# A gated layer in blocks of 1024 rows, with the seven-product form for the down product too

## The chip, the cores and the metric

One core of a Trainium2 chip runs the kernel. The metric is the device time in microseconds (us). Before the change it is 1163.14 us, the median of three runs (1162.55 to 1168.49). The engines are TensorE (PE in the profile; PEld is its weight load), VectorE (DVE), ScalarE (ACT), GpSimd (POOL) and SyncE (SP), whose queue issues nearly all DMA transfers.

## What is computed

Two layers, each an FNet mixing (a real part of a two-dimensional DFT by matrices) and a gated unit. S is 2048, D is 640, F is 1728.

```python
def _A_ref(x, dft_seq_re, dft_seq_im, dft_hid_re, dft_hid_im):
    a = jnp.einsum("bsd,ed->bse", x, dft_hid_re)
    b = jnp.einsum("bsd,ed->bse", x, dft_hid_im)
    return jnp.einsum("ts,bse->bte", dft_seq_re, a) - jnp.einsum("ts,bse->bte", dft_seq_im, b)

def _B_ref(x, w_gate, w_up, w_down):
    g = jnp.einsum("bsd,df->bsf", x, w_gate)
    u = jnp.einsum("bsd,df->bsf", x, w_up)
    return jnp.einsum("bsf,fd->bsd", _sigmoid(g) * u, w_down)

x = A_x
x = x + _A_ref(_layernorm(x), ...)
x = x + _B_ref(_layernorm(x), B_w_gate, B_w_up, B_w_down)
x = x + _A_ref(_layernorm(x), ...)
x = x + _B_ref(_layernorm(x), B_w_gate, B_w_up, B_w_down)
```

## The kernel before

**Numbers.** Every fp32 operand is split into two fp16 parts, HI and LO, and a product takes three matmuls (HI by HI, HI by LO, LO by HI: `PASSES`). The split is one ScalarE instruction (HI) and one VectorE instruction (LO).

**Mixing.** `sequence` and `hidden` use the symmetries of the DFT matrices ("folds" of the rows and columns, `fold_...`), so that mixing is short. That the matrices have these symmetries is tested while the kernel runs: `load_rows`, `load_cols` fetch pieces of the matrix into one of two rooms, `test_rows` and `test_cols` (VectorE, lines 1299, 1300, 1302 and 1316 on) subtract, and `square_rest` (ScalarE, line 1277) sums the squares. At the end a flag is set, and if it is bad, a second general program runs. `test_w` also checks the range of the weights.

**Gated unit.** The 2048 rows are taken in four blocks of 512 (`SB`). The first block in each layer is plain: `gate_up(b, j)` computes a tile of 128 columns of gate and up, 30 matmuls of 512 columns (line 1051), for each of 13 tiles j and a tail of 64 + 64 columns. The other three blocks use a form of Strassen and Winograd: halves of 256 rows and the two sets gate and up give a 2 by 2 product, computed in seven products instead of eight. `seven(b, j)` runs it for two tiles j and j + 1 side by side, each part for the one and then for the other (54 matmuls of 256 columns a tile, in `products`, line 1097; the tail is line 1180). The sums of weights (`make_sums`, GpSimd, lines 998 to 1001) are made once and kept in DRAM; the sums of rows are made by `pair_combine` on VectorE. Three of the products share one PSUM chain: `snap` (ScalarE, line 1101) copies the running sum out between them, before the next one adds to the same bank. VectorE adds the sums (1133, 1134), ScalarE takes the sigmoid (1143), VectorE multiplies (1153, 1155), and ScalarE and VectorE split the result (1164, 1165).

**Down.** `down` computes 128 rows by 640 columns, in two halves of 320, over all of F: 82 matmuls of 320 columns (line 1244) for 128 rows. VectorE adds the result to the rows (line 1259), and in the second layer they are stored.

**Memory and order.** Everything lies in one SBUF tensor `big`, in units of 128 columns. Some tiles have fixed places; the rest come from `Slots`, which picks, among a few free places, the one that was freed longest ago. A step is a group of matmuls; every other piece of work is put at a step by hand (`at(u, f, ...)`), and each engine executes its own list in that order, waiting only for what it needs. The opening has an order of its own (`OPENING`).

Of the kernel before, what the change touches and what calls it, by code (L numbers as in the profile page):

```python
# [16 lines left out]
P = 128  # L17
S = 2048
# [29 lines left out]
WMAX = 16.0  # L48
# [12 lines left out]
UNITS = 388  # L61
# [5 lines left out]
XTU = NT * 2  # L67
WDU = (NF + 1) * 5
FIX = XU + 2 * XTU + WDU


class Slots:

    LOOK = {4: 2, 5: 6}

    def __init__(self, big):
        self.big = big
        self.live = {}  # L80
        self.freed = {}
        self.clock = 0
        self.close = False

    def take(self, n, high):
        taken = sorted(self.live.values())
        if self.close:

            ends = [FIX] + [d for _, d in taken]
            free = [(a, b) for a, b in zip(ends, [c for c, _ in taken] + [UNITS]) if a + n <= b]  # L90
            assert free, f"no room for {n}: {taken}"
            if high:
                a = [a for a in range(UNITS - n, FIX - 1, -n) if all(a + n <= c or d <= a for c, d in taken)][:high]
                if a:
                    return self.new(min(a, key=lambda a: max(self.freed.get(u, 0) for u in range(a, a + n))), n)
                a = max(b for _, b in free) - n
            else:
                a = min((a for f in free for a in {f[0], f[1] - n}),
                        key=lambda a: (max(self.freed.get(u, 0) for u in range(a, a + n)), a))
            return self.new(a, n)  # L100
        found = []
        for i in range(UNITS):
            a = UNITS - (i + 1) * n if high else FIX + i * n
            if a < FIX or a + n > UNITS:
                break
            if all(a + n <= c or d <= a for c, d in taken):
                found.append(a)
                if len(found) == self.LOOK.get(n, 3):
                    break
        if not found:  # L110
            found = [a for a in range(FIX, UNITS - n + 1) if all(a + n <= c or d <= a for c, d in taken)][:1]
        assert found, f"no room for {n}: {taken}"
        age = lambda a: max(self.freed.get(u, 0) for u in range(a, a + n))
        return self.new(min(found, key=age), n)

    def new(self, a, n):
        s = Slot(self.big[:, a * UNIT : (a + n) * UNIT], (a, a + n))
        self.live[id(s)] = s.span
        return s

    def give(self, s):
        self.clock += 1
        del self.live[id(s)]
        for u in range(*s.span):
            self.freed[u] = self.clock


class Slot:
# [9 lines left out]
PASSES = ((HI, (HI, LO)), (LO, (HI,)))  # L138

# [27 lines left out]
    wshi 0 0, evhi 1 1 1, wld 4 0, ev 1 1 2, ev 1 1 1, wshi 0 1, hid 0 1, hid 1 0, evhi 1 1 0, wslo 0 1, ev 1 1 0,  # L167
    difhi 1, hid 2 1, dif 1, hid 2 0, sum 0, add 0, wshi 4 0, nst 0, sum 1, nst 1, hidev 1 0, hidev 2 0, npow 0,
    add 1, wld 4 1, hid 3 1, nst 2, nst 3, nscale 0, hid 1 1, nrm 0, nrm 1, nhi 0, nhi 1, hidev 3 1, nlo 0,
    hidev 1 1, nlo 1, wld 3 1, tp 0, wslo 2 1, tp 1, wslo 0 0, npow 1, tpl 0, tpl 1, nscale 1, mid, tph 1, tph 0,  # L170
    hidev 2 1, wld 3 0, wshi 3 1, nrm 2, nhi 2, wslo 2 0, nlo 2, gu 0 0, tp 2, gu 1 0, nrm 3, wslo 3 1, tpl 2,
    tph 2, midhi, middif, nhi 3, wshi 4 1, nlo 3, tp 3, wslo 4 0, tph 3, wslo 4 1, gu 2 0, tpl 3, wshi 3 0,
    wslo 3 0, gu 0 1, gu 1 1, gu 2 1"""
# [24 lines left out]
def folded(ctx, tc, pool, dram, big, acc, flag, x, ct, wh, wg, wu, wc, wd, out):  # L198
# [4 lines left out]
    half = pool.tile([P, 4], F32, name="half")  # L203
# [3 lines left out]
    small = [pool.tile([P, 2, 24], F32, name=f"small{i}") for i in range(8)]  # L207
# [7 lines left out]
    turn = [0]  # L215
    n_sum, n_max = [0], [0]

    def scratch():
        turn[0] += 1
        return small[turn[0] % len(small)]  # L220

    nc.vector.memset(half, -0.5)
# [17 lines left out]
    def start():  # L240
        nc.gpsimd.memset(dsum, 0.0)
        nc.gpsimd.memset(cmax, 0.0)

# [12 lines left out]

    steps = []
    jobs = defaultdict(list)

    def at(u, f, *a):  # L260
        jobs[max(0, int(u // 1))].append((u, f, a))
# [3 lines left out]
    def take(n, *key, high=False):  # L265
        key = key if len(key) > 1 else key[0]
        assert key not in held, key
        held[key] = slots.take(n, high)
        return held[key]

    def fixed(at, n, *key):

        assert key not in held, key
        held[key] = Slot(big[:, at * UNIT : (at + n) * UNIT], None)
        return held[key]

    def drop_fixed(*key):
        del held[key]
# [56 lines left out]
    def load_x(i, g):  # L335

        turned = g in (GB, GC)
        v = fixed(FIX - WDU + 10 * i + 5 * (g - GB), 5, "xr", i, g).f32 if turned else X[:, 4 * i + g, :]
# [23 lines left out]
    def turned_squares(i, g):  # L362
# [3 lines left out]
        drop_fixed("xr", i, g)  # L366
# [22 lines left out]
    stats = {}  # L389
# [6 lines left out]
    def rstd_power(t, n, on=nc.gpsimd):  # L396
        c = [t[:, :n, k] for k in range(24)]
        on.tensor_scalar(c[14], c[13], 1.0, EPS, op0=OP.mult, op1=OP.add)
        nc.gpsimd.tensor_tensor(c[15], c[14], half[:, :n], op=OP.pow)
# [18 lines left out]
    def norm_scale(r, n=1, on=nc.gpsimd):  # L418
        t = stats.pop((r, n))
        rstd(t, n, XS, on)  # L420

    def norm_stats_act(r):

        t, junk = stats[r], take(5, "junk").f32
# [5 lines left out]
    def norm_pair(r):  # L430
        t = stats[r, 2] = scratch()
        for q in range(2):
            stats[r + q] = t[:, q, :]

    def norm_stats_dve(r):
        t = stats[r]
        for h in range(2):
            nc.vector.bn_stats(t[:, 6 * h : 6 * h + 6], X[:, r, h * EH : (h + 1) * EH])
        nc.vector.bn_aggr(t[:, 12:14], t[:, 0:12])

    def norm_apply(r, on_act=False):
        t = stats.pop(r)

        xn = fixed(XU + XTU + 10 + 5 * r, 5, "xf", r).f32
# [1366 lines left out]
```

## Time and profile before

| | |
|---|---|
| median of the runs | 1163.14 us |
| the profiled execution, first to last instruction | 1160.1 us |
| TensorE busy | 97% |
| VectorE busy | 64% |
| ScalarE busy | 44% |
| GpSimd busy | 13% |
| DMA, mean | 187 GB/s, 216.40 MB |

The profile is of one execution. A grouped line names the line of the kernel, the engine, the operation, output and input, shapes, the count, the busy time in us, the mean of one in ns, and the idle time before it with what ended it. A row of the windows gives, for a stretch of time, the busy us and the count of PE, PEld, DVE, ACT and POOL, the granted clock (1.00 is full), the mean busy share of the DMA engines and what they moved in GB/s. Matmuls overlap, so the mean ns of one is not the time from one to the next.

### The profile page before, as it was taken

Reading aid. Unit: us, or ns where it says so; the run is one execution under the profiler, and the core shown is the slowest. Engines: PE = TensorE matmul, PEld = TensorE weight load, DVE = VectorE, ACT = ScalarE, POOL = GpSimd, SP = SyncE. Lnnn points to the kernel's source line nnn. Section 1 sums busy time; section 2 is a strip of 40 time slices with the busy share of each in tenths; the row PEclk is TensorE's granted clock in tenths of the full one; section 3 lists DMA queues with packets and bytes.
Section 4 is the critical chain, followed back from the end, with each engine's and each line's share of the span. In section 5 each row is a group of like instructions: output and inputs, shape, how many; then the busy total and the mean of one; then the engine's idle time right before and its main releaser. Section 6 shows DMA issues by size and latency. Waiting matters only on the chain.

```text
span 1160.1 us, 22627 instructions
## 1 busy us (share of the span) xinstructions
PE 1127.3 (97%) x8784; PEld 859.6 (74%) x8784; DVE 737.6 (64%) x1636; ACT 508.2 (44%) x1094; POOL 147.6 (13%) x269
## 2 busy tenths in 40 slices
PE   6699999999999999999999999999999999999997
PEld 2467446788878887888776744678887888788874
DVE  7996888768748666685428557747974557525530
ACT  6864575155515653365204312325542555225410
POOL 2312674201002010100000001000100001000000
PEclk9999999999999999999999999999999999999999
DMA  8418698959596977679203552678859682767301
GB/s 278 136 46 242 243 358 267 280 163 234 156 222 185 242 215 187 199 236 261 70 24 108 189 150 81 185 230 251 245 155 252 205 282 93 168 207 246 115 18 38
DMA packets 225621, 216.40 MB, mean 187 GB/s; under 512 B 68034, under 2 KB 181851, under 8 KB 225502
## 3 DMA queue, kind: packets, MB, share of 16 engines
q1 hardware_dynamic: 224862, 212.23, 62.3%
q0 software_dynamic: 640, 2.62, 0.6%
q8 instruction: 71, 1.16, 0.4%
q14 instruction: 48, 0.39, 0.1%
HBM read 171.03 MB, written 30.40 MB: 174 GB/s over the span
## 4 chain that ended last, share of the span: by engine, by line
PE 81%; DMA 3%; POOL 2%; DVE 1%; issue 1%; ACT 1%; SPq 0%; POOLq 0%; DVEq 0%; ACTq 0%
PE acc L1097 36%; PE acc L1244 31%; PE acc L1051 8%; PE acc L855 2%; PE acc L1180 2%; PE acc L773 1%; DMA big<-kept_w 1%; DMA big<-in_ct 1%; POOL big L999 1%; POOL big L1000 1%; DMA kept_s<-big 1%; DVE big L238 0%; POOL big L998 0%; POOL big L1001 0%; DMA big<-kept_s 0%
## 5 line engine op out<-in xcount | busy, mean ns | idle before, releaser
L1097 PE MATMUL acc<-big 128*128 128x256 f16 x4212 | 462.9, 273 | 1.4 <-DVE small L416 1.4
L1097 PEld LDWEIGHTS <-big 128*128 128x128 f16 x4212 | 411.9, 98 | 49.9 <-DMA big<-kept_w 1.7
L1244 PE MATMUL acc<-big 128*128 128x320 f16 x2624 | 357.7, 299 | 0.0
L1244 PEld LDWEIGHTS <-big 128*128 128x128 f16 x2624 | 256.8, 98 | 99.7
L1101 ACT ACTIVATE big<-acc 128x256 f32<-128x256 f32 x312 | 116.1, 381 | 200.1 <-PE acc L1097 198.5
L1051 PE MATMUL acc<-big 128*128 128x512 f16 (+1 forms) x990 | 176.5, 340 | 0.6 <-ACT big L236 0.4
L1051 PEld LDWEIGHTS <-big 128*128 128x128 f16 x990 | 96.5, 98 | 79.6 <-ACT big L236 0.8
L1277 ACT ACTIVATE big<-big 128x768 f32<-128x768 f32 (+8 forms) x104 | 79.4, 764 | 130.4 <-DVE big L1302 94.8
L1165 DVE TENSOR_TENSOR big<-big 128x512 f16<-128x512 f32 x78 | 53.8, 690 | 110.7 <-ACT big L1164 110.7
L1259 DVE SCALAR_TENSOR_TENSOR big<-acc,big 128x320 f32<-128x320 f32 x64 | 28.4, 484 | 88.3 <-PE acc L1244 88.2
L238 DVE SCALAR_TENSOR_TENSOR big<-big 128x640 f16<-128x640 f32 (+6 forms) x81 | 64.5, 834 | 2.8 <-ACT big L236 2.2
L1143 ACT ACTIVATE big<-big 128x512 f32<-128x512 f32 x78 | 47.9, 627 | 39.2 <-DVE big L1134 39.1
L1299 DVE TENSOR_TENSOR big<-big 128x256 f32<-128x256 f32 x64 | 26.6, 416 | 52.6 <-DMA big<-in_ct 51.3
L236 ACT ACTIVATE big<-big 128x640 f16<-128x640 f32 (+7 forms) x81 | 50.7, 665 | 17.0 <-DMA kept_s<-big 7.7
L1134 DVE TENSOR_TENSOR big<-big,acc 128x512 f32<-128x512 f32 x78 | 53.1, 681 | 3.2 <-PE acc L1097 3.0
L1153 DVE SCALAR_TENSOR_TENSOR big<-acc,big 128x256 f32<-128x256 f32 x78 | 32.6, 418 | 33.4 <-PE acc L1097 28.4
L1164 ACT ACTIVATE big<-big 128x512 f16<-128x512 f32 x78 | 48.8, 626 | 7.8 <-DVE big L1155 6.8
L855 PE MATMUL acc<-big 128*128 128x321 f16 (+3 forms) x324 | 49.0, 300 | 1.1 <-DVE big L238 1.1
L855 PEld LDWEIGHTS <-big 128*128 128x128 f16 (+3 forms) x324 | 28.2, 95 | 20.3 <-issue 7.7
L509 ACT ACTIVATE big<-big 128x384 f16<-128x384 f32 (+2 forms) x48 | 28.9, 647 | 31.4 <-DVE big L491 17.6
L1066 DVE SCALAR_TENSOR_TENSOR big<-acc,big 128x512 f32<-128x512 f32 x26 | 17.9, 687 | 35.0 <-PE acc L1051 28.5
L773 PE MATMUL acc<-big 128*128 128x256 f16 (+5 forms) x288 | 36.9, 288 | 2.6 <-DVE big L664 2.6
(183 smaller groups left out, 978.7 us busy)
## 6 DMA issues: line engine op xcount, KB each, us to landing
big<-kept_w SPq DMA_DIRECT2D x125, 320.0 KB
big<-kept_s SPq DMA_DIRECT2D x75, 512.0 KB
big<-in_ct SPq DMA_DIRECT2D x256, 128.0 KB
big<-kept_w SPq DMA_DIRECT2D x78, 192.0 KB
kept_w<-big SPq DMA_DIRECT2D x41, 320.0 KB
big<-in_ct SPq DMA_DIRECT2D x32, 256.0 KB
kept_s<-big SPq DMA_DIRECT2D x13, 512.0 KB
big<-in_wg SPq DMA_DIRECT2D x16, 320.0 KB
```

The costliest lines, as they stand in the source:

```text
L236: nc.scalar.activation(dh, src, AF.Copy, scale=s)
L238: nc.vector.scalar_tensor_tensor(dl, src, s, dh, op0=OP.mult, op1=OP.subtract)
L773: nc.tensor.matmul(o, xv[:, 384 * xp + c0 : 384 * xp + c0 + n], moving(r, cps[cp]), start=(i % 2 == 0 and r == 0 and xp == HI and cp == HI ...
L855: nc.tensor.matmul(ps[:m, :EC], z[:, at : at + m], w[:, 384 * wp : 384 * wp + EC], start=(d == 0 and zp == HI and wp == HI), stop=(d == ND ...
L1051: nc.tensor.matmul(ps, w[wp][:, d * P : (d + 1) * P], xt[:, xp, :], start=(d == 0 and wp == HI and xp == HI), stop=(d == ND - 1 and wp == LO))
L1097: nc.tensor.matmul(ps, wt, xt, start=start and n == 0, stop=n == len(todo) - 1, skip_group_check=not start)
L1101: nc.scalar.activation(dst, ps, AF.Copy)
L1134: nc.vector.tensor_tensor(v, v, other, op=OP.add)
L1164: nc.scalar.activation(s.parts[HI], v, AF.Copy)
L1165: nc.vector.tensor_tensor(s.parts[LO], v, s.parts[HI], op=OP.subtract)
L1244: nc.tensor.matmul(held["pd", e][0][:, :EH], held["ht", j].parts[hp][:, i * P : (i + 1) * P], held["w", 2, j].parts[wp][:, e * EH : (e + 1 ...
L1277: nc.scalar.activation(v, v, AF.Square, accum_out=new_sum()[:p])
```

## The change

1. **Blocks of 1024 rows.** There are two blocks; in the seven-product form the halves have 512 rows, so each of the seven products is a series of matmuls of 512 columns. Column tiles j = 0 to 5 of the first block are still plain (`JC`), for both halves; tiles 6 to 12 of the first block and all 13 of the second are in the form. `seven(j)` is six steps and `four(j)` a seventh, which comes in the midst of the next tile. That makes 20 tiles in the form for each layer.
2. **Three downs in the form.** In the first block of the first layer `down` stays as it was in arithmetic. In the other three, pairs of column tiles (6 pairs of F), the halves of rows and the two halves of 320 columns give a 2 by 2 product. It runs product by product: `stage(h, s, i)` is product s of 7 for 128 rows, 18 matmuls of 320 columns; the rest of F (tile 12 and the tail) adds 5 for each 128 rows by 320 columns. The sums of the down weights are made on GpSimd (`make_forms`), split, and kept in DRAM in the first layer; the sums of activations are made by VectorE (`sums_of`) and GpSimd (`third_sum`), and each product's factor is split (`split_form`).
3. **Row pairs.** `pair_combine` of the second block is on GpSimd. Transposed rows have one buffer (`XW`), not two.
4. **Places.** No tile but the rows has a fixed place; every `take` gets the next number of a table, `PLACES`.
5. **Order.** Steps carry a duration, and other work is put at a time (`when(t, f, ...)`) on the sum of these durations.
6. **Tests.** Three rooms in place of two, loaded two turns ahead and not one; a row of a piece has 256 columns, not 128. The range of most weights is tested where they are first loaded, in the first layer, and the upper bound is 4, not 16.

The diff, cut to its core:

```diff
-WMAX = 16.0
+WMAX = 4.0
+JC = 6
+PLACES = """
+311 389 198 205 250 365 289 115 268 85 207 357 321 147 295 91 341 180 106 362 217 97 225 220 352 336 101 255
...
+    def take(self, n):
+        a = self.places.pop(0)
...
-    def part_one(b, j):
-        chain, kc = bank()
-        other, ko = bank()
-        chain = chain[:, :256]
...
+    def seven(j):
+        def one():
+            held["chain", j] = bank()
+            products(held["chain", j][0], j, [("G0", "x00")], start=True)
+        def one_post():
+            snap(take(4, "y", 0, j).f32, held["chain", j][0])
+        def five():
+            held["other", j] = bank()
+            products(held["other", j][0], j, [("S1", "T1")], start=True)
+        def five_post():
+            take(8, "hw", j)
+            snap(hw(1), held["other", j][0])
+        def two():
+            held["first", j] = bank()
+            products(held["first", j][0], j, [("G1", "x01"), ("GM", "x0M")], start=True)
+        def two_post():
+            ps, k = held.pop(("first", j))
+            nc.vector.tensor_tensor(hv(0), hv(0), ps, op=OP.add)
+            free_bank(k)
+            due(2, lambda: sigmoid(hv(0)))
+        def six():
+            products(held["chain", j][0], j, [("S2", "T2")])
...
+        return [(n * 0.2158, f, g) for n, f, g in ((6, one, one_post), (6, five, five_post), (9, two, two_post),
+                                                   (6, six, six_post), (9, three, three_post), (9, seven, seven_post))]
...
+    def make_forms(n):
+        b12, b11, b21, b22 = (held["fr", n].f32[:, k * EH : (k + 1) * EH] for k in range(4))
+        v = take(10, "ft", n).f32
+        t1, t3, t2, t4 = (v[:, k * EH : (k + 1) * EH] for k in range(4))
+        nc.gpsimd.tensor_tensor(t1, b12, b11, op=OP.subtract)
+        nc.gpsimd.tensor_tensor(t3, b22, b12, op=OP.subtract)
+        nc.gpsimd.tensor_tensor(t2, b22, t1, op=OP.subtract)
+        nc.gpsimd.tensor_tensor(t4, b21, t2, op=OP.subtract)
+        absmax(wmax[:, 2, n : n + 1], held["fr", n].f32)
...
+    TAKES = ((0, 0), (0, 1), (0, 0), (1, 0), (0, 1), (1, 0), (1, 1))
+    INTO = (("chain", 0), ("other", 0), ("other", 3), ("chain", 1), ("other", 1), ("chain", 3), ("chain", 2))
+    REST = {1: 0, 4: 1, 6: 2}
...
+    def stage(h, s, i, final):
+        into, k = INTO[s]
+        fresh = s in (0, 1, 2)
+        def mm():
+            half, second = TAKES[s]
+            if fresh:
+                held[into, "d", i] = bank()
+            ps = held[into, "d", i][0]
...
+            if s in REST:
+                rest_products(ps, REST[s] // 2, i, REST[s] % 2, False)
+        def post():
...
+            rows_add(h, k // 2, i, k % 2, ps)
+            if s in (1, 4, 6):
+                del held[into, "d", i]
+                free_bank(bk)
```

Two places show how instructions have moved. The first is ScalarE's list in the seven-product form of the first layer, beside the folds of the second quarter of rows. Before (1101 is a snap, 1164 the HI part of a result, 621 and 623 are folds, 1277 a squaring of a test, 1143 the sigmoid):

```order
L1101 ACTIVATE big<-acc_69 128x256
L1101 ACTIVATE big<-acc_65 128x256
L1164 ACTIVATE big<-big 128x512
L621 ACTIVATE big<-big,coef_89,quad_77 128x321
L623 ACTIVATE big<-big,quad_77 128x320
L1277 ACTIVATE big,dsum<-big 128x768
L1101 ACTIVATE big<-acc_67 128x256
L1101 ACTIVATE big<-acc_346 128x256
```

After, in the second block of the first layer (1112 is a snap, 1115 the sigmoid, 1415 a squaring, 240 the HI part of a form of the down weights, 624 and 626 are the folds):

```order
L1112 ACTIVATE big<-acc_65 128x512
L240 ACTIVATE big<-big 128x3x320
L1415 ACTIVATE big,dsum<-big 128x768
L1112 ACTIVATE big<-acc_69 128x512
L240 ACTIVATE big<-big 128x4x320
L1115 ACTIVATE big<-big 128x512
L1415 ACTIVATE big,dsum<-big 128x768
L1112 ACTIVATE big<-acc_69 128x512
L624 ACTIVATE big<-big,coef_86,quad_77 128x321
L626 ACTIVATE big<-big,quad_77 128x320
L1112 ACTIVATE big<-acc_66 128x512
```

Snaps have twice the columns, stand one by one, and have splits of the forms and squarings between them. The second place is VectorE's list there. Before (1133, 1134 are sums of products, 1299, 1300, 1302 a test, 1153, 1155 the products of gate and up, 1165 a LO part):

```order
L1133 TENSOR_TENSOR big<-big 128x256
L1134 TENSOR_TENSOR big<-big,acc_346 128x512
L1299 TENSOR_TENSOR big<-big 128x256
L1300 TENSOR_TENSOR big<-big 128x256
L1302 TENSOR_TENSOR big<-big 128x128 x2
L1153 SCALAR_TENSOR_TENSOR big<-acc_69,big 128x256
L1155 SCALAR_TENSOR_TENSOR big<-big 128x256
L1165 TENSOR_TENSOR big<-big 128x512
```

After (1158, 1173, 1185 are sums of products, 1188 and 1202 the products of gate and up, 1336 is a sum for the down form, 1445, 1446, 1448 a test, 667 a fold, 242 the LO part of a form):

```order
L1158 TENSOR_TENSOR big<-big,acc_65 128x512
L1188 SCALAR_TENSOR_TENSOR big<-big 128x512
L1336 TENSOR_TENSOR big<-big 128x512 x2
L1445 TENSOR_TENSOR big<-big 128x256
L1446 TENSOR_TENSOR big<-big 128x256
L1448 TENSOR_TENSOR big<-big 128x128 x2
L1202 SCALAR_TENSOR_TENSOR big<-acc_64,big 128x512
L667 TENSOR_TENSOR big<-big 128x2x321
L667 TENSOR_TENSOR big<-big 128x2x320
L242 SCALAR_TENSOR_TENSOR big<-big 128x4x320
L1173 TENSOR_TENSOR big<-big,acc_66 128x512
L1336 TENSOR_TENSOR big<-big 128x512
```

The sums for the down form and the LO parts of the forms of the weights have joined the list between the additions that free PSUM banks (1158, 1173, 1202).

1187 lines of the change are left out of this document (656 added, 531 removed), and 31 rows, old and new, of the table PLACES.

## The prediction

> **What bounds the kernel now.** I read the page's first table, then TensorE's own waits, then the chain that ended last, then the grouped lines.
>
> ```profile
> span 1160.1 us, 22627 instructions
> PE 1127.3 (97%) x8784; PEld 859.6 (74%) x8784; DVE 737.6 (64%) x1636; ACT 508.2 (44%) x1094; POOL 147.6 (13%) x269
> ...
> PE twin L350 <- ACT big L356: 12.1, 6, 7.7
> ...
> PE acc L1097 <- DVE small L416: 1.4, 1, 1.4
> ```
>
> TensorE (PE) is the bound. Its waits are those of the opening, and one of 1.4 us later on (engine, line, releaser, total us, times, longest). The opening ends where the matmuls of L1051 become dense, and from there the chain of waits is nearly TensorE alone:
>
> ```profile
> 96.28 43.91 PE L1051 MATMUL acc<-big 128*128 128x256 f16 x262
> ...
> 178.49 44.55 PE acc L1244 x328
> 223.04 71.39 PE acc L1097 x654
> 294.43 1.64 PE acc L1180 x15
> ...
> 650.33 81.20 PE acc L1051 x435
> ```
>
> These rows (start, us, what) give the price of one matmul in a stream, which the 273 and 299 ns of the grouped lines do not, since matmuls overlap. 71.39 / 654 = 0.1092 us for 256 columns; 44.55 / 328 = 0.1358 us for 320; in the last row 120 of the 435 have 256 columns and 315 have 512 (counted from the loops), so (81.20 - 120 x 0.1092) / 315 = 0.2162 us for 512. Twice the columns cost 1.98 times as much: wider tiles alone save almost nothing, and only columns that are no longer computed do.
>
> **The change on TensorE.** The counts of before:
>
> ```profile
> L1097 PE MATMUL acc<-big 128*128 128x256 f16 x4212 | 462.9, 273 | 1.4 <-DVE small L416 1.4
> L1244 PE MATMUL acc<-big 128*128 128x320 f16 x2624 | 357.7, 299 | 0.0
> L1051 PE MATMUL acc<-big 128*128 128x512 f16 x630 | 136.6, 379 | 0.6 <-ACT big L236 0.4 <-DVE big L238 0.3
> L1180 PE MATMUL acc<-big 128*128 128x256 f16 x216 | 25.5, 273 | 0.0
> ```
>
> Downs: before 2624 matmuls of 320 columns. After: the first block of the first layer stays plain (656), the other three take 28 stages of 18 and 16 x 5 for the rest, 584 each. That is 2408, and 216 x 0.1358 = 29.3 us are gone.
> Gates and ups: gone are 4212 + 216 of 256 columns and 90 of the 630 of 512 (483.5 + 19.5 = 503.0 us). New are 40 products of 54 and four times two tails of 15, 2280 of 512 columns (492.9 us). That saves 10.1 us: one plain column tile fewer in each layer, and shorter tails.
> Together 39.4 us. The opening keeps its matmuls; its wait stays.
> [...]
>
> **What TensorE may wait for.** In the seven-form, three products pass through one PSUM chain and ScalarE (ACT) copies the running sum (a snap) before TensorE adds the next. Before, snaps had 256 columns, now 512:
>
> ```profile
> L1101 ACT ACTIVATE big<-acc 128x256 f32<-128x256 f32 x312 | 116.1, 381 | 200.1 <-PE acc L1097 198.5
> L1065 ACT ACTIVATE big<-acc 128x512 f32<-128x512 f32 x26 | 15.4, 592 | 46.4 <-PE acc L1051 22.2 <-DVE big L1076 21.7 <-POOL big L1000 2.4
> ```
>
> After the first part, parts five and two run on other banks: 15 x 0.2162 = 3.24 us, against a snap of 0.59. It is free while less than 2.6 us stands ahead of it on ScalarE. The other two crossings have 18 matmuls or more behind them, but for a block's first product.
> Bank frees on VectorE (DVE): eight banks, three taken for each 11.7 us product; that hides several us of lag. Down stages: the last adds onto a bank that VectorE must have read after the stage before, 28 matmuls of 0.1358 us (3.8 us) earlier; such a reading addition is 0.48 us (L1259).
>
> ```profile
> L1259 DVE SCALAR_TENSOR_TENSOR big<-acc,big 128x320 f32<-128x320 f32 x64 | 28.4, 484 | 88.3 <-PE acc L1244 88.2
> ```
>
> **The fullest stretch** is the first layer's second block: 13 products and two tails, 732 x 0.2162 = 158 us. Into it fall tests of the DFT matrix, the forms of the down weights and the folds.
>
> ```profile
> L1134 DVE TENSOR_TENSOR big<-big,acc 128x512 f32<-128x512 f32 x78 | 53.1, 681 | 3.2 <-PE acc L1097 3.0
> L1300 DVE TENSOR_TENSOR big<-big 128x256 f32<-128x256 f32 x64 | 26.9, 421 | 16.9 <-DMA big<-in_ct 16.7
> L1302 DVE TENSOR_TENSOR big<-big 128x128 f32<-128x128 f32 x128 | 31.7, 290 | 2.2
> L238 DVE SCALAR_TENSOR_TENSOR big<-big 128x768 f16<-128x768 f32 x13 | 13.4, 1031 | 0.0
> ...
> 129.94 2.75 DVE L238 SCALAR_TENSOR_TENSOR big<-big 128x640 f16<-128x640 f32 x4
> ...
> 150.12 1.35 DVE L238 SCALAR_TENSOR_TENSOR big<-big 128x640 f16<-128x640 f32 x1
> ...
> 158.20 0.81 DVE L238 SCALAR_TENSOR_TENSOR big<-big 128x640 f16<-128x640 f32 x1
> ```
>
> VectorE has 297 instructions there: 99 of 512 columns (0.69: 68 us), 68 of 256 (0.42: 29), 48 of 128 (0.29: 14), 18 of the forms with 960 or 1280 columns (26, an estimate from 1.03 us for 768), and 64 of the folds and the rest (30): 167 us. Neighbours overlap: four of 0.81 took 2.75, so 0.85 of the sum, 142 us of 158. It fits, at 90%. GpSimd (POOL) runs 24 additions of forms in it, and beside it a VectorE instruction took 1.35 instead of 0.81: if each of the 24 meets one, 13 us, and VectorE is at 98%. I take a loss of 3 us for TensorE; bounds 0 and, in the rivals, 9.
> DMA moves 42.3 MB in it (180 transfers: 15.6 tests, 11.6 gate weights, 6.9 forms written, 4.0 raw down weights, 4.2 others), 268 GB/s. Last columns here, DMA share and GB/s:
>
> ```profile
> 348.16:430.35 82.19, 80.74 (x740) 72.12 (x739) 58.71 (x150) 45.48 (x107) 11.01 (x30) 1.00 0.79 209
> 474.90:555.46 80.56, 80.56 (x740) 72.12 (x739) 56.03 (x135) 45.53 (x105) 4.57 (x13) 1.00 0.83 237
> 390.00:420.00 30.00, 28.55 (x262) 25.36 (x261) 21.69 (x59) 16.85 (x40) 5.13 (x16) 1.00 1.03 232
> 150.00:180.00 30.00, 29.39 (x141) 13.45 (x140) 25.59 (x34) 23.82 (x46) 21.62 (x31) 1.00 0.99 370
> ```
>
> Full engines gave 232 to 370 GB/s, by the mix. At 237 / 0.83 = 286 the stretch needs 148 us, hidden; at 232 it needs 182. The tests' row loads now take 256 columns at a time, not 128, which favours the upper figures. Gate weights are ordered some 15 us ahead. I take 1 us.
> Opening: some 10 us of VectorE work (the second quarter's rows: joins, adds, statistics) join its end, where VectorE came to stand idle:
>
> ```profile
> 103.08 0.69 DVE L1066 SCALAR_TENSOR_TENSOR big<-acc,big 128x512 f32<-128x512 f32 x1 [4.11 <-PE acc L1051]
> ```
>
> The first matmuls that need this work come three column tiles, 90 x 0.2162 = 19 us, after the last early half tile. Cost 0, bounds 0 and 3. Into the second layer the folds have 16.7 us of other matmuls ahead of the sequence that needs them: 1 us, bounds 0 and 3.
> Tail:
>
> ```profile
> 1146.52 5.90 SPq L382 DMA_DIRECT2D out<-big  x2
> 1151.57 0.49 DVE L1259 SCALAR_TENSOR_TENSOR big<-acc,big 128x320 f32<-128x320 f32 x1 [5.08 <-PE acc L1244]
> ```
>
> From 1152.06 to 1160.1 the last store lands, 160 KB. Now it is 320 KB: between 0 and 0.9 us more (160 KB at the mean of 187 GB/s); I take 0.9.
> **Sum:** 1160.1 - 39.4 + 3 + 1 + 1 + 0.9 = 1126.6 us of span. The median of the runs, 1163.14, lies 3.0 above the span, so 1129.6; rounded, 1129.
>
> **Rivals.**
> 1. *VectorE or the DMA fills the stretch* and TensorE waits for weights or banks. VectorE: an addition of 320 columns on GpSimd is 0.91 us by the 0.73 that 256 columns took undisturbed; 24 of these blocked in full are 22 us, 142 + 22 = 164, and with a lost wait or two 167, 9 over the 158. DMA at 232 GB/s: 182 - 158 = 24 over. That puts the time at 1129 - 4 + 9 to 24 = 1134 to 1149. For it: TensorE lost 1.45 us in the window at 1.03. Against: that window was the only one.
>
> ```profile
> 120.69 0.72 POOL L1000 TENSOR_TENSOR big<-big 128x256 f32<-128x256 f32 x1
> 146.19 1.19 POOL L1000 TENSOR_TENSOR big<-big 128x256 f32<-128x256 f32 x1
> ...
> DVE big L1299 <- DMA big<-in_ct: 51.3, 15, 7.5
> ACT big L1277 <- DVE big L1302: 94.8, 22, 9.7
> ```
>
> [...]
> 2. *Slower: snaps stand behind work that waits.* ScalarE takes its queue in order. A squaring of a test (L1277) waited 94.8 / 22 = 4.3 us for VectorE on average, 9.7 at most, and VectorE in turn for test data. With 4.3 + 1.0 for the squaring + 0.6 for the snap, part six comes 5.9 - 3.2 = 2.7 us late. One such in each of 40 products is 107 us: 1129 - 4 + 107 = 1232. It decides the sign from 15 products on (39.4 / 2.7). For it: a snap of one product is no longer followed by the partner product's parts, and squarings and splits of forms stand between snaps. Against: those waits were of a ScalarE that idled at 44%, in the same mix of snaps and squarings TensorE never waited for L1101, and tests now have three rooms and two paces of lead where they had two and one.
> 3. *The change does not save what it says:* the wide stream runs slower than 315 matmuls of it did. 2280 at 0.233 us instead of 0.216 give 39 us back, and the time stays at 1163. Only the 0.379 us of the grouped line for 512 columns could speak for it, and that counts overlapping time.
>
> **How the numbers follow.** Forecast (1118 to 1133) 0.68; rival 1 (1134 to 1150) 0.15; rival 2 (from 1170, half of it up to 1232) 0.12; rival 3 0.05. The lower end is the sum without any loss, 1160.1 - 39.4 - 1.4 + 3 = 1122, less 5 for what the opening may give: 1117. The upper end, 1152, takes in rival 1. About 0.5% (6 us) is what a measurement of this kernel tells from no change, so faster means below 1157: 0.84; same 0.05, from rival 3 and the edge of rival 2; slower 0.11.
>
> **What would show it.** Right: 2280 matmuls of 512 columns in the seven-form at 0.216, TensorE's busy time near 1088 us, its waits after 110 us together under 8 us, VectorE above 85% in the first layer's second block. Rival 1: waits of TensorE on weights there, DMA share at 1. Rival 2: matmuls of the seven-form waiting for snaps, some 2 to 3 us, in many products. The forecast is wrong if the matmul rate falls or if waits recur with every product.

## The result and the profile after

The changed kernel takes 1173.32 us (median of four runs, 1171.05 to 1174.1) against 1162.85 us before (four runs, 1162.21 to 1168.49). The ratio is 1.0081, 95% interval 1.0057 to 1.0106: about 10 us slower, where 34 us faster was forecast. The top of the profile after, then the mean clock of the changed kernel and of the kernel before:

```profile
span 1172.3 us, 17676 instructions
PE 1101.6 (94%) x6330; PEld 622.1 (53%) x6330; DVE 839.7 (72%) x1642; ACT 577.3 (49%) x1117; POOL 206.9 (18%) x295
```
```profile
core 0: 1172.3 us, clock 0.986
```
```profile
core 0: 1160.1 us, clock 0.998
```

TensorE is busy for 25.7 us less than before, not 39.4, and idle for 38 us more (70.7 and 32.8). Three groups of the chain of waits show first that the price of a matmul is not the cause (start, us, what):

```profile
168.58 79.64 PE acc L1108 x369
...
272.82 67.64 PE acc L1250 x497
...
1108.72 22.00 PE acc L1364 x162
```

79.64 / 369 = 0.2158 us for 512 columns, 67.64 / 497 = 0.1361 and 22.00 / 162 = 0.1358 for 320. So the loss can be laid out over the whole trace: for each matmul, the distance from its start to the next start, less the price of its columns. Before, the last matmul ends at 1151.5 and 32.5 us of it are lost: 1119.0 of work. After, it ends at 1165.8 with 86.1 lost: 1079.7. The saving is there, 39.3 us. (Work in this sense is count times price, so the rows above, and not this difference, test the price.) The saving was lost again: 53.6 us more are lost than before, 49.4 of them at four new places:

| TensorE's lost time, us | before | after |
|---|---|---|
| opening | 28.1 | 27.8 |
| start of the first layer's second block | 0.0 | 5.1 |
| its seven-product form, the stretch from 350 to 525 us | 1.6 | 20.2 |
| between the layers | 2.9 | 5.0 |
| second layer, downs of the first block | 0.0 | 13.7 |
| second layer, end of the seven-product form | 0.0 | 12.0 |
| the rest | -0.1 | 2.3 |

TensorE's own waits after, the longest behind the opening (engine, line, releaser, total us, times, longest):

```profile
PE acc L1108 <- ACT big L1112: 15.6, 9, 4.5
...
PE acc L1108 <- DMA big<-kept_G: 6.1, 2, 4.4
PE acc L1364 <- DVE big L1238: 4.7, 3, 4.0
...
PE acc L1108 <- DMA big<-big: 3.2, 1, 3.2
PE acc L1345 <- DVE big L1238: 2.9, 1, 2.9
```

Nine times a product waits for a snap (L1112), twice for gate weights, four times a down stage for VectorE, once a product for a transpose; before there was one such wait, of 1.4 us. These are 32.5 us, and smaller ones come on top. Another 13.6 us are the clock, which in this trace falls to half after some of the waits (1.00, then 0.51 and 0.50 below). A table of windows of 3.41 us around the longest wait (start and end, length, busy time and count of PE, PEld, DVE, ACT and POOL, granted clock, DMA share, GB/s):

```profile
391.75:395.16 3.41, 3.41 (x17) 1.57 (x16) 3.27 (x4) 1.00 (x1) 2.98 (x5) 1.00 0.53 192
395.16:398.57 3.41, 0.20 (x1) 0.00 (x0) 3.38 (x9) 1.67 (x3) 0.00 (x0) 1.00 0.55 187
398.57:401.98 3.41, 2.12 (x6) 0.73 (x6) 3.38 (x6) 3.03 (x5) 0.00 (x0) 0.51 0.51 166
401.98:405.40 3.42, 3.42 (x10) 1.18 (x9) 3.39 (x8) 1.42 (x3) 0.00 (x0) 0.50 0.66 191
405.40:408.80 3.40, 3.40 (x17) 1.58 (x16) 3.40 (x6) 1.72 (x3) 0.00 (x0) 0.99 0.97 351
```

The wait empties one window, and the next two run at half clock: 10 matmuls of 512 columns in 3.42 us instead of 16 or 17. Between the opening and the last matmul there are eight such half windows, 8 x 3.41 / 2 = 13.6 us, which is what PE's busy time has over the 1088 that was forecast.

**Where the weights come late** (second layer, around 1040 us). SP's queue in order of time, then TensorE:

```profile
1037.37 12.09 SPq L1499 DMA_DIRECT2D big<-in_wh  x4
1049.56 3.14 SPq L1037 DMA_DIRECT2D big<-kept_G  x1
...
1053.75 12.29 SPq L1499 DMA_DIRECT2D big<-in_wh  x4
```
```profile
1060.76 9.63 PE L1108 MATMUL acc<-big 128*128 128x512 f16 x36 [4.44 <-DMA big<-kept_G]
```

Four loads of hidden-matrix rows for a test keep SP busy for 12 us, and the gate weights of the next product stand behind them. They stand behind them once more on the DMA engines: of the 128 packets of these gate weights 112 have landed by 1054.8 us, and the other 16, an eighth, start only at 1059.4 and end at 1060.3, just before the product starts. In the window 1046.50 to 1049.30 nothing but such a load is under way, and the mean busy share of the DMA engines is 0.13 (row in experiment 1): 2.1 of 16.

**Where the snaps come late** (first layer, second block). ScalarE in order of time:

```profile
388.28 0.60 ACT L1112 ACTIVATE big<-acc 128x512 f32<-128x512 f32 x1 [0.16 <-PE acc L1108]
391.83 1.00 ACT L240 ACTIVATE big<-big 128x960 f16<-128x960 f32 x1 [2.96 <-DMA big<-in_wd]
395.18 1.49 ACT L662 ACTIVATE big<-big 128x642 f16<-128x642 f32 x2 [2.35 <-DVE big L660]
398.39 0.84 ACT L1415 ACTIVATE big<-big 128x768 f32<-128x768 f32 x1 [1.71 <-DVE big L1448]
399.14 0.19 ACT L1415 ACTIVATION_READ_ACCUMULATOR big<-big 128x1 f32 x1
399.23 0.58 ACT L1112 ACTIVATE big<-acc 128x512 f32<-128x512 f32 x1
```

Between two snaps stand a split of a down form that waits for its raw weights, a fold that waits for VectorE, and the squares of a test that wait for VectorE. VectorE had its own waits for the same raw weights (the list of all waits):

```profile
DVE wmax L233 <- DMA big<-in_wd: 22.0, 5, 8.0
...
ACT big L240 <- DMA big<-in_wd: 11.3, 4, 6.8
```

**Where a place is reused too soon** (second layer, downs of the first block):

```profile
880.14 0.92 ACT L442 ACTIVATE big<-big,rowt 128x640 f32<-128x640 f32 x1 [17.27 <-DMA big<-big]
```

The third row tile of the next block is normalised into a place from which a transpose by DMA still reads the second tile. ScalarE stands 17 us before this instruction, with the factors of the next down product (L1324) behind it.

### The profile page after: what moved, and what is told of

Same layout as the page of the kernel before. It is cut to its first block, busy times and chain, and to the rows that moved or that the text cites. A ratio compares the mean times of both kernels' runs of the same rounds, so it can differ in the third digit from the quotient of the medians.

```text
span 1172.3 us, 17676 instructions
## 1 busy us (share of the span) xinstructions
PE 1101.6 (94%) x6330; PEld 622.1 (53%) x6330; DVE 839.7 (72%) x1642; ACT 577.3 (49%) x1117; POOL 206.9 (18%) x295
## 4 chain that ended last, share of the span: by engine, by line
PE 67%; DMA 15%; DVE 11%; ACT 3%; issue 2%; SPq 1%; POOL 1%; DVEq 0%; ACTq 0%
PE acc L1108 26%; PE acc L1364 14%; PE acc L1064 11%; PE acc L1250 6%; PE acc L858 4%; DMA big<-in_wh 4%; DMA big<-in_ct 3%; PE acc L1345 2%; DMA big<-big 2%; PE acc L776 2%; DVE big L242 1%; PE acc L1217 1%; DMA big<-kept_U 1%; DVE big L1325 1%; DMA big<-kept_f 1%
## 5 line engine op out<-in xcount | busy, mean ns | idle before, releaser
L1108 PE MATMUL acc<-big 128*128 128x512 f16 x2160 | 477.5, 383 | 25.1 <-ACT big L1112 15.6
L1108 PEld LDWEIGHTS <-big 128*128 128x128 f16 x2160 | 212.8, 99 | 288.3 <-issue 33.0
L1364 PE MATMUL acc<-big 128*128 128x320 f16 x1512 | 216.5, 301 | 7.9 <-DVE big L1238 4.7
L1364 PEld LDWEIGHTS <-big 128*128 128x128 f16 x1512 | 148.9, 99 | 68.8 <-issue 7.6
L1112 ACT ACTIVATE big<-acc 128x512 f32<-128x512 f32 x160 | 93.5, 590 | 147.5 <-PE acc L1108 147.2
L1064 PEld LDWEIGHTS <-big 128*128 128x128 f16 x900 | 87.8, 98 | 67.9 <-issue 0.6
L1325 DVE TENSOR_TENSOR big<-big 128x512 f16<-128x512 f32 x126 | 93.9, 760 | 19.1 <-ACT big L1324 18.9
L1250 PE MATMUL acc<-big 128*128 128x320 f16 x656 | 89.6, 299 | 1.2 <-DVE big L242 0.8
L242 DVE SCALAR_TENSOR_TENSOR big<-big 128x640 f16<-128x640 f32 (+7 forms) x94 | 77.7, 850 | 12.6 <-ACT big L240 12.6
L1324 ACT ACTIVATE big<-big 128x512 f16<-128x512 f32 x126 | 72.0, 616 | 14.8 <-DVE big L1325 7.9
L1250 PEld LDWEIGHTS <-big 128*128 128x128 f16 x656 | 64.2, 98 | 26.6 <-POOL big L1019 1.0
L240 ACT ACTIVATE big<-big 128x640 f16<-128x640 f32 (+8 forms) x94 | 63.5, 705 | 28.2 <-DMA big<-in_wd 11.3
L1339 POOL TENSOR_TENSOR big<-big 128x512 f32<-128x512 f32 x18 | 28.4, 1602 | 250.5 <-DVE big L1325 249.4
L507 ACT ACTIVATE big<-big 128x384 f16<-128x384 f32 (+2 forms) x56 | 36.6, 667 | 51.5 <-DVE big L492 12.4
L508 DVE TENSOR_TENSOR big<-big 128x384 f16<-128x384 f32 (+2 forms) x56 | 45.7, 825 | 20.2 <-ACT big L507 13.3
L1158 DVE TENSOR_TENSOR big<-big,acc 128x512 f32<-128x512 f32 x40 | 27.3, 682 | 41.9 <-PE acc L1108 36.0
```

Source lines behind the costliest of these rows:

```text
L240: nc.scalar.activation(dh, src, AF.Copy, scale=s)
L242: nc.vector.scalar_tensor_tensor(dl, src, s, dh, op0=OP.mult, op1=OP.subtract)
L1064: nc.tensor.matmul(ps, w[wp][:, d * P : (d + 1) * P], xt[:, xp, :], start=(d == 0 and wp == HI and xp == HI), stop=(d == ND - 1 and wp == LO))
L1108: nc.tensor.matmul(ps, wt, xt, start=start and n == 0, stop=n == len(todo) - 1, skip_group_check=not start)
L1112: nc.scalar.activation(dst, ps, AF.Copy)
L1250: nc.tensor.matmul(held["pd", i, e][0][:, :EH], held["t", half, j].parts[hp][:, i * P : (i + 1) * P], held["w", 2, j].parts[wp][:, e * EH ...
```

## The experiments

All but the eleventh change the kernel after the change. The numbers of TensorE's lost time are worked out from each trace as above; where an edit changes the order, each tile keeps its place and the table is only written in the new order. Numbers 1 to 8, 11 and 12 are one run each, 9 and 10 are four; the kernel before alone ranged from 1162.2 to 1168.5 us, so a single run is read by its trace more than by its time.

**1. Hidden rows in ten pieces.**

```diff
-            nc.sync.dma_start(v[:, g, :EH], bass.AP(wh.tensor, (r * D + row) * D, [[EH, 2], [d * D, 64], [1, EH]]))
+            nc.sync.dma_start(v[:, g, :EH].rearrange("p (n c) -> p n c", c=64),
+                              bass.AP(wh.tensor, (r * D + row) * D, [[64, 10], [d * D, 64], [1, 64]]))
```

> The changed kernel's loads of hidden-matrix rows for the test (L1499) were moved by two DMA engines at a time (128 packets of 1280 bytes, 3.8 us each load); here each load is cut into ten columns of 64, so that ten engines take part. Theory (weights stand behind these loads in SP's queue): TensorE's losses between 1040 and 1087 us of the changed kernel, 12.1 us with the half clock that follows them, shrink to under 2 us, and the span goes from 1172 to about 1161. Rival (the gate and up weights are late for their own sake, since the queue holds too much there): the losses stay, 1170 to 1174.

Measured: span 1189.6, time 1191.4, and 31.9 us lost at that place instead of 12.0. Both theories missed. The loads became slower (SP is busy for 15.1 us with four, not 12.1), and what stands behind them came later: that they hold up the weights is shown by the wrong sign. Three windows tell why, each with hardly anything but hidden rows under way: of this run, of the changed kernel, and of the kernel before.

```profile
1036.00:1047.00 11.00, 7.33 (x26) 2.61 (x24) 2.29 (x4) 2.20 (x5) 0.00 (x0) 0.84 0.16 36
```
```profile
1046.50:1049.30 2.80, 2.80 (x15) 1.27 (x14) 0.00 (x0) 0.95 (x2) 0.00 (x0) 1.00 0.13 49
```
```profile
1024.00:1029.00 5.00, 5.00 (x45) 4.10 (x42) 1.49 (x3) 1.40 (x4) 0.00 (x0) 1.00 0.38 112
```

The shares are 0.16 for ten pieces, 0.13 for two (the change), 0.38 for five pieces of 80 rows into 100 partitions (before): 2.6, 2.1 and 6.1 of 16. Ten pieces kept hardly more of the engines busy than two.

**2. Matrix rows as before, in 16 pieces of 128 columns.**

```diff
-        v = room().rearrange("p (g c) -> p g c", g=4)
+        v = room().rearrange("p (g n c) -> p g n c", g=4, n=2)
...
-            nc.sync.dma_start(v[:, g], bass.AP(ct.tensor, (r * S + row) * S, [[256, 8], [d * S, 16], [1, 256]]))
+            nc.sync.dma_start(v[:, g], bass.AP(ct.tensor, (r * S + row) * S, [[P, NS], [d * S, 16], [1, P]]))
```

> The loads of matrix rows for the test (L1439) are undone to the form of before: 16 outer pieces of 128 columns, not 8 of 256. Theory A (a load that only 8 of the 16 DMA engines carry holds up the raw down weights behind it): TensorE's losses between 390 and 512 us, 20 us, fall to under 10, span 1160 to 1165. Theory B (the raw weights are late because they are asked for only 5 us ahead): the losses stay within 5 us of 20, span 1168 to 1175. Theory C (VectorE is full in that stretch): the same as B.

Measured: span 1158.8, time 1160.6. This is what theory A says, and 1.2 us more: the stretch loses 9.4 us instead of 20.2, the start of the block 1.3 instead of 5.1. The 9.4 that stay leave room for the other two theories. A window with hardly any other transfer has share 0.55 in the changed kernel (395.16 to 398.57, above) and of 1.23 here (above 1: on average 1.23 x 16 = 19.7 packets were under way at once):

```profile
385.00:387.00 2.00, 2.00 (x11) 0.91 (x10) 2.00 (x4) 1.29 (x2) 1.10 (x3) 1.00 1.23 253
```

VectorE's wait for the raw down weights falls from 22.0 to 9.2 us.

**3. Sums of the down weights later.**

```diff
-                when(u + 5, make_forms, n)
+                when(u + 9.5, make_forms, n)
...
-                    when(u + 9 + 5 * k, split_forms, n, k)
-                    when(u + 12 + 5 * k, keep_forms, n, k)
+                    when(u + 13 + 4.5 * k, split_forms, n, k)
+                    when(u + 15.5 + 4.5 * k, keep_forms, n, k)
```

> The sums of the down weights are made 4.5 us later after their load is asked for, and their splits and stores 3 to 4 us later; nothing else moves. Theory B (raw weights asked for 5 us ahead and landing after 7 to 10 us make VectorE and ScalarE wait, and the snaps behind them): the waits for in_wd (22 us of VectorE, 11 us of ScalarE) fall to under 8 together, TensorE's losses between 390 and 512 us from 20 to under 8, span 1158 to 1164. Theory C (VectorE is full there): the waits only change their name, losses 15 to 25, span 1168 to 1176.

Measured: span 1167.8, time 1169.6; 17.6 us lost in the stretch instead of 20.2. VectorE's waits for raw weights fell to 5.6 us and ScalarE's from 11.3 to 1.1, as theory B has it, but TensorE kept its losses, as C has it. One new wait came with the edit: ScalarE's split stands 5.2 us for a store of an earlier form. More lead alone does not bring the loss back.

**4. Row tiles of the second layer later.**

```diff
-            u = d0 + 2 + 20 * i if first else d0 + 11 + 15 * i
+            u = d0 + 2 + 20 * i if first else d0 + (11, 26, 50, 60)[i]
```

> In the second layer the third and fourth tile of the second block's rows are normalised 9 and 4 us later, so that ScalarE does not reach this work before the transposes by DMA of the second tile, whose place it writes, have landed. Theory (ScalarE waits 17 us for that landing with the factors of the next down product behind it): TensorE's losses between 875 and 900 us, 13 us, fall to under 4; up to 5 us may come back at the start of the second block, since the last transpose is later; span 1162 to 1169. Rival (the down stage waits for VectorE, which is late anyway): losses stay, span 1170 to 1175.

Measured: span 1165.4, time 1167.3; 6.8 us lost there instead of 13.7, and nothing came back at the start of the block. The mechanism is shown, but 6.9 us were gained where over 9 were expected. What is left is the wait behind it: three loads for the next down product stand, as before the edit, behind the second transpose, which SP takes 6.61 us to issue.

**5. Hidden rows in sixteen pieces.** As 1, with `c=40` and `[[40, 16], [d * D, 64], [1, 40]]`.

> Ten outer pieces made the loads of hidden rows slower, not faster (about 2.5 packets under way at a time, as with two pieces). [...] Then 16 pieces of 40 columns run on 16 engines in spite of their short packets of 160 bytes: a load takes under 1.5 us, the weights behind it come in time, TensorE's losses at the end of the second layer's seven-product form (12 us) fall to under 2, span 1160 to 1163. Rival (the length of the packets decides): 1024 packets of 160 bytes are slower still than the 640 of 256, span above 1190.

Measured: span 1161.1, time 1162.9; the 12.0 us are gone (-0.1). SP's queue now, and a window with little else under way than hidden rows:

```profile
1015.33 8.83 SPq L1499 DMA_DIRECT2D big<-in_wh  x4
1024.25 0.61 SPq L1037 DMA_DIRECT2D big<-kept_G  x1
...
1037.90 9.56 SPq L1499 DMA_DIRECT2D big<-in_wh  x4
```
```profile
1028.00:1035.00 7.00, 7.00 (x34) 3.17 (x33) 2.79 (x5) 2.53 (x5) 0.00 (x0) 1.00 0.59 114
```

The gate weights behind the loads are issued in 0.61 us, not 3.14, and all their 128 packets land within 1.5 us. The loads themselves did not become as short as expected: SP takes 8.83 / 4 = 2.2 us to issue one, where 1.5 were expected. But short packets of 160 bytes, spread wide (0.59, or 9.4 of 16 engines on average), beat packets of 1280 bytes with a share of 0.13. In engines of 16, the shares measured in these runs are 2.1 for 2 pieces, 2.6 for 10, 6.1 for 5 (into 100 partitions), 8.8 for 8, and for 16 pieces 9.4 here and 19.7 in number 2, with overlapping packets and some other transfers in them. So the number of pieces alone does not decide: ten got 2.6. What does decide is not shown, and that 16 pieces would use all 16 engines was the author's estimate.

**6. to 8. The three together, with the forms later, and with the tests spread.** Number 6 is 2, 4 and 5; 7 adds 3; 8 is 6 with

```diff
-        spans = [(d0 + 6, e0, 0.6), (e0, d1, 1.0), (d1, d1 + 40, 0.4)] if first
+        spans = [(d0 + 6, e0, 0.8), (e0, d1, 0.75), (d1, d1 + 60, 0.6)] if first
```

> Three edits together: matrix rows in 16 pieces, hidden rows in 16 pieces, and the third and fourth row tile of the second layer's second block later. If the causes are separate places, the gains add up: 13.5 (matrix rows), 11 (hidden rows), 7 (row tiles) from 1172.3, span 1138 to 1144. If one took over another's losses, 1145 to 1155.

> The same three, and the sums of the down weights 4.5 us later after their load. If late raw weights still cause what is left between 350 and 510 us (9.5 us beside the row loads in 16 pieces), another 4 to 8 us go: 1132 to 1138. If VectorE, 90% busy there, is the cause, no change to e6 within 3 us.

> The three edits of e6, and the tests of the first layer spread more evenly: about 54% of them in the seven-product stretch of the second block, not 71%, the rest in the down stages before and after. If VectorE's fill of that stretch (143 us of 160) is what is left there, the 9.5 us fall to under 4: 1132 to 1137, and nothing comes back in the down stages. If it is late raw weights, no change to e6 within 3 us.

Measured: spans 1140.7, 1141.4 and 1142.6; times 1142.5, 1143.2 and 1144.4. The gains of the three places add up. In the stretch 13.1, 13.7 and 6.0 us are lost: the later forms do nothing, and fewer tests halve it, so much of what was left comes with the tests, be it by their work on VectorE and ScalarE or by their loads. But number 8 loses 9.4 us at the start of the block, where SP issues eight row loads of the tests, 10.98 us, ahead of the last transpose, and gains nothing over all.

**9. and 10. All of it, the late transpose earlier; and the sums of row pairs back on VectorE.** Number 9 is 8 with weights 0.7, 0.75, 0.8, and

```diff
-            u = d0 + 2 + 20 * i if first else d0 + (11, 26, 50, 60)[i]
+            u = d0 + ((2, 22, 42, 57) if first else (11, 26, 54, 63))[i]
...
-                when(u + 4 + 2 * n, pair_parts, 1, i, n)
+                when(u + 4 + (2 if first or i < 2 else 1.5) * n, pair_parts, 1, i, n)
-            when(max(u + 13, d0 + (45 if first else 37) + i), pair_transpose, 1, i, 0)
+            when(max(u + (13 if first or i < 2 else 10), d0 + (45 if first else 37) + i), pair_transpose, 1, i, 0)
```

and number 10 is 9 with `on = nc.vector` in `pair_combine`.

> The edits of e6 and the spread tests of e8 (weights 0.7, 0.75, 0.8 over the down stages before, the seven-product form, and the stages behind), with the fourth row tile of the first layer's second block 5 us earlier (its transpose came late in e8: 9.4 us lost), and in the second layer the third tile another 4 us later and the fourth 3 us later with its parts closer together. Expected: the 9.4 us of e8 fall to under 3, the 3.8 us in the second layer's down stages to under 2, the stretch stays at 6: span 1128 to 1135, the time 1130 to 1137. If the transposes are late because the queue and the engines are full, and not by their place in the order, 1138 to 1144.

> e9 with the sums of row pairs of the second block on VectorE again, as before the change, not on GpSimd. If the transposes wait for these sums behind the weight sums on GpSimd, another 1 to 4 us go at the end of the first down stage; if not, VectorE has 16 more additions in two stretches where it is 60 to 85% busy, and the time stays within 3 us of e9.

Measured: 9 takes 1134.44 us (1132.26 to 1136.77), 0.9748 of the kernel before (interval 0.972 to 0.9777); 10 takes 1133.63 us, 0.9738 (0.9713 to 0.9762). Both beat both kernels; the place of the sums makes no difference. The page of 9, and its waits of TensorE behind the opening:

```profile
span 1131.1 us, 17721 instructions
PE 1087.8 (96%) x6330; PEld 619.3 (55%) x6330; DVE 839.5 (74%) x1642; ACT 576.9 (51%) x1117; POOL 209.8 (19%) x295
```
```profile
PE acc L1108 <- ACT big L1112: 6.4, 5, 2.7
...
PE acc L1364 <- DVE big L1238: 3.6, 3, 2.0
```

The instructions of TensorE are those of the changed kernel, and PE's busy time is the 1088 us that was forecast: until the last matmul there is no half window left. That is in part luck, since two waits of 2.6 and 2.9 us remain, and number 10 has one half window after a wait of 2.6. 6.4 us are lost in the stretch and 8.0 between the layers (5.0 in the changed kernel; the tests that were moved behind the stretch now stand there, which is the likely reason).

**11. The kernel before with rows in 8 pieces.** The edit of 2 the other way round, in the kernel before.

> The kernel before, with only its loads of matrix rows in 8 pieces of 256 columns, as the change has them. If such a load is costly wherever it stands, the kernel before loses several us too (1168 to 1180). If it costs only where weights and raw weights stand close behind it with little lead, as in the changed kernel, no change within 4 us of the kernel before.

Measured: 1172.2 us beside 1162.4 for the kernel before on the same chip, span 1170.3. Behind the opening TensorE loses 11.7 us instead of 4.4, 4.4 us of it in two waits for weights that the kernel before does not have:

```profile
PE acc L1097 <- DMA big<-kept_w: 4.4, 2, 3.1
```

So in this run the narrow load alone is worth 7.3 us even where nothing else has changed; 2.7 us are differences of the opening, before the first such load.

**12. No tests in the stretch.**

```diff
+            if first and e0 < at_test(n) < d1 - 10:
+                continue
```

> The three edits of e6, and the first layer's tests that fall into the seven-product form of the second block left out altogether (their loads, VectorE's subtractions, ScalarE's squares). If VectorE's fill, with the tests in it, is all that is left of TensorE's losses there (13 us in e6), they fall under 2 and the span to 1126 to 1131. If the forms of the down weights and the folds alone still hold up the snaps, 4 us or more stay.

Measured: span 1128.3, time 1130.2, and nothing lost in the stretch (-0.2 us, 13.1 in number 6). Its windows, those of number 9, and those of the changed kernel:

```profile
350.00:505.00 155.00, 155.00 (x720) 70.28 (x719) 116.84 (x179) 74.94 (x125) 36.86 (x48) 1.00 0.60 192
```
```profile
350.00:505.00 155.00, 149.13 (x689) 67.19 (x687) 138.88 (x261) 86.75 (x156) 36.90 (x48) 1.00 0.87 249
```
```profile
350.00:525.00 175.00, 159.86 (x707) 70.42 (x707) 142.97 (x282) 95.06 (x173) 34.50 (x48) 0.96 0.78 243
```

With VectorE at 75% (116.84 of 155) and the DMA engines at 0.60, forms and folds hold nothing up. With it at 90%, 6 us are lost. How much of that is VectorE's work and how much the loads of the tests stays open, since 12 takes away both. The trace of number 9 shows that VectorE's fill is not all. Its two longest losses in the stretch, 2.6 us after 419 and 2.9 after 481, make up 5.5 of the 6.4. These rows of ScalarE, and one of VectorE, stand ahead of the snaps that TensorE waited for there:

```profile
420.81 0.66 ACT L624 ACTIVATE big<-big,coef,quad 128x321 f32<-128x321 f32 x1 [2.90 <-POOL coef L613]
477.61 1.00 ACT L240 ACTIVATE big<-big 128x960 f16<-128x960 f32 x1 [4.75 <-DMA big<-in_wd]
481.82 0.63 ACT L1324 ACTIVATE big<-big 128x512 f16<-128x512 f32 x1 [3.21 <-DMA big<-kept_S]
```
```profile
477.59 1.49 DVE L233 TENSOR_REDUCE wmax<-big 128x1 f32<-128x1280 f32 x1 [6.29 <-DMA big<-in_wd]
```

Ahead of the one a fold waits 2.90 us for a coefficient from GpSimd. Ahead of the other both engines stand for raw down weights, VectorE for 6.29 us, and then ScalarE stands another 3.21 us, by the profile for sums of weights (kept_S); VectorE's work that it needs ends at nearly the same time. In number 12 neither engine waits for raw weights in this window.

TensorE's lost time of these runs, in us (7 and 11 are told above, and 10 is close to 9):

| run | block start | stretch | between layers | downs, layer 2 | end of form, layer 2 | span |
|---|---|---|---|---|---|---|
| after | 5.1 | 20.2 | 5.0 | 13.7 | 12.0 | 1172.3 |
| 1 | 2.0 | 20.9 | 5.0 | 12.9 | 31.9 | 1189.6 |
| 2 | 1.3 | 9.4 | 5.0 | 14.1 | 12.5 | 1158.8 |
| 3 | 3.5 | 17.6 | 5.0 | 13.4 | 12.3 | 1167.8 |
| 4 | 4.9 | 20.0 | 5.0 | 6.8 | 12.4 | 1165.4 |
| 5 | 5.2 | 21.7 | 5.0 | 13.3 | -0.1 | 1161.1 |
| 6 | 1.2 | 13.1 | 5.0 | 5.4 | -0.1 | 1140.7 |
| 8 | 9.4 | 6.0 | 7.1 | 3.8 | -0.1 | 1142.6 |
| 9 | 0.0 | 6.4 | 8.0 | 0.4 | -0.1 | 1131.1 |
| 12 | 1.2 | -0.2 | 6.6 | 4.7 | -0.1 | 1128.3 |

Numbers 2 and 6 have the same edit in the stretch and lose 9.4 and 13.1 us there, so differences of some 4 us between single runs say little.

## Why the prediction was wrong, point by point

- **The saving on TensorE, 39.4 us, was right**, and so was the price of 0.216 us that it rests on. The third rival (a slower stream) is refuted: 0.2158 us in the new form.
- **DMA in the full stretch: the step that failed first, a term of 1 us.** The prediction put 42.3 MB into it, which is right (243 GB/s for 175 us, 42.5 MB). It then said that row loads of 256 columns instead of 128 favour the upper figures of GB/s, which no row showed, and took 1 us. The runs show the reverse: with 8 outer pieces the share was 0.55, or 8.8 of 16 engines, with 16 it was 1.23, and VectorE waited 22.0 us for the raw weights behind the former and 9.2 behind the latter. Undoing this alone gives 13.5 us of span (number 2), and giving it to the kernel before costs 7.3 (number 11). The row loads were costed by bytes, and not by how their access pattern spreads. 3.8 of the 13.5 us lie at the start of the block, ahead of the stretch.
- **The hidden rows were not in the sum at all.** Four loads with a share of 0.13 of the DMA engines stand ahead of gate weights that were taken as ordered 15 us ahead: 12.0 us, all of which number 5 gives back.
- **VectorE in the full stretch: the sum was right, the conclusion was not.** Forecast 142 us of work, measured 143.0. The 13 or 22 us that additions on GpSimd might have cost it are not seen in that. No run shows the full blocking behind the 22 us, and so behind the 9 of the first rival's range; the 143.0 measured here are 1 us above the sum without any. "It fits, at 90%" with a loss of 3 us fails: a mean says nothing of what stands in line at one moment, and a snap that is late by more than its cover stops TensorE. With the loads of rows in 16 pieces 13.1 us are still lost at 88% (number 6, 140.8 of 160 us), with the tests spread 6.4 (number 9), and none without tests, at 75% (number 12). How much of this is VectorE's work, and how much the tests' loads, stays open.
- **The second rival had the mechanism, not the size, and by itself it would not have turned the sign.** Snaps do stand behind work that waits, 15.6 us in nine waits, seven of them among the 13 products of the full stretch, and not 2.7 us in each of 40. Ahead of six of the seven stands the squaring of a test, and ahead of three a split that waited for raw weights. The price per place was fair (1.7 us on average, without the half clock), the number of places far too high. The first rival's 9 to 24 us for the stretch hold its 20.2, but in part by luck: its upper figure supposes full DMA engines, and their share was 0.78.
- **Transposes were not costed.** A row tile of the second block is now one transpose of 34 tiles, 5 to 8 us to issue on SP, and its place is reused at once: 13.7 us in the second layer (with the order of number 9, a later third and fourth tile, 0.4 are left). The 5.1 at the start of the block are a wait for a transpose as well, but number 2 takes 3.8 of them away, so there the narrow row loads make it late.
- **The half clock was not costed.** Eight half windows are 13.6 us, a quarter of the 53.6 that were lost again. Waits of 2 us and more were priced at their own length.
- **Opening, between the layers, tail.** The opening lost 27.8 us, as before. Between the layers 2.1 us were added where 1 was taken. The tail is 6.5 us long from the last matmul, not 0.9 longer than the 8.6 of before. The median lies 1.0 above the profiled span, not 3.0.

So the sum fails by the four places, of which it put the stretch at 4 us and left out the other three. With them mended, and the tests spread, the same instructions of TensorE take 1131.1 us of span, 4.5 above the 1126.6 of the forecast, and the time of 1134.4 lies within its range.

## What to carry to other kernels

Price a DMA by the share of the engines that loads of its access pattern keep busy in a trace, and not by its bytes: here an outermost count of 16 on the source side, into 128 partitions, was worth 11 to 14 us at each of two kinds of load, even at the cost of short packets. In a kernel whose main engine has no slack, ask for each in-order queue (SP's as well) what stands directly ahead of the work that the main engine waits for, and whether that itself waits; a mean fill of 90% is no proof that it fits. A wait of some 2 us can cost nearly twice its length (2.2 us and 1.7 of half clock in the windows below), where half clock follows it.

## What the runs showed of the hardware

- In the changed kernel's trace TensorE's granted clock holds for whole windows of 3.41 us: one with 0.20 us of work is followed by half clock (above), and one with 1.37 us of 3.40 as well. With 1.83 and 1.93 of 3.40 it stays at 1.00, though a wait of 3.2 us lies across these two. The next rows are of the changed kernel, the last two of number 10:

```profile
432.70:436.10 3.40, 1.37 (x7) 0.58 (x6) 3.40 (x6) 3.15 (x8) 0.27 (x1) 1.00 0.84 235
436.10:439.60 3.50, 3.50 (x10) 1.18 (x8) 3.47 (x10) 2.77 (x7) 0.00 (x0) 0.51 0.92 323
460.00:463.40 3.40, 1.83 (x9) 0.73 (x8) 3.37 (x8) 1.51 (x6) 0.00 (x0) 1.00 0.61 220
463.40:466.80 3.40, 1.93 (x9) 0.87 (x9) 3.40 (x6) 2.80 (x6) 0.00 (x0) 1.00 1.01 305
466.80:470.30 3.50, 3.50 (x18) 1.60 (x17) 3.46 (x8) 2.19 (x5) 1.93 (x2) 1.00 0.77 269
```
```profile
420.80:424.20 3.40, 0.95 (x5) 0.38 (x4) 3.37 (x7) 1.59 (x3) 1.36 (x2) 0.99 1.05 350
424.20:427.60 3.40, 3.40 (x10) 1.21 (x8) 3.37 (x9) 3.23 (x7) 0.00 (x0) 0.50 1.06 324
```

- The windows of this trace do not start with the waits. Half clock sets in at 350.8, 398.6, 436.2, 883.3, 897.0 and 1060.8 us, which lie 14, 11, 131, 4 and 48 windows of 3.413 us apart. So what a wait cost here depended on where it fell: 2.2 us within one window cost another 1.7, and 3.2 us across two cost nothing more.

- The issue of what stands behind narrow transfers on SP's queue was slower as well: the same load of gate weights took 3.14 us to issue behind four loads of hidden rows in two pieces (changed kernel) and 0.61 behind four in 16 (number 5).
